# Attention scores and values side by side in 64x32 tiles of the matmul array

## The chip, the cores and the metric

The kernel runs on one core of a Trainium2 chip. The core has a matmul engine (TensorE, "PE" in the profile), three engines that read and write on-chip memory (VectorE "DVE", ScalarE "ACT", GpSimd "POOL") and a queue that issues DMA transfers (SyncE, "SP"). TensorE multiplies a stationary operand, loaded by an instruction of its own ("PEld", LDWEIGHTS), with a moving operand that streams through, and writes to PSUM, which has eight banks of 128 partitions x 512 float32. The metric is device time in microseconds (us), lower is better, as the median of several executions.

## The reference

The input x has 2048 rows of 640 features. Two attention blocks, A and B, with weights of their own, run on the same x; each has 32 heads of 20 features. A gate per row mixes the two results:

```
q, k, v = (x @ wqkv) split into 3 x 32 heads x 20
scores  = q @ k.T * 20 ** -0.5
p       = softmax(scores)
block   = (p @ v, heads side by side) @ wo
g       = sigmoid((x * gate_w).sum(-1))
out     = g * A + (1 - g) * B
```

## The kernel before

**Units of work.** The 64 heads of both blocks are taken in 16 groups of four (index g). A group has four blocks of 512 queries (qb), and each of these is worked off in eight steps of 256 keys. That makes `STEPS` = 16 x 4 x 8 = 512 steps, counted by G.

**Number formats.** Queries and keys stand as float16 in two parts (a high part and a remainder), so that a head takes 60 rows of 64: the rows of head pair members 0 and 1 lie in partitions 0 to 63 and 64 to 127 of the tiles `QT` and `KT`. Rows 60 to 63 carry the maximum of the scores of each query, subtracted inside the product. Values `V` and the weights of the softmax (`pt`) are float32.

**What a step does.** For step G the kernel issues

- scores (`scores`, "e" in the order below): 8 matmuls of 64 rows x 128 keys, with 512 queries moving (L696), each into a PSUM bank of its own; ScalarE takes the exponential of each bank into a `pt` tile (L699);
- maxima (`max_mm`, "m"): the same product the other way round for queries that come 15 steps later (`LEAD`): 8 matmuls of 60 rows x 128 queries with 512 keys moving (L638). VectorE reduces each bank to a maximum per query (L649). For one bank in eight, ScalarE first writes a part (L642), and VectorE combines it with another bank (L646);
- values (`values`, "V"), for the step before: two blocks, each of four float32 matmuls of 128 keys x 21 columns with 512 queries moving (L714). The four heads go to four column tiles of 32 columns and add up in one bank, `acc`;
- other products ("X", `slot`): the projections of the next groups (`project_a`, `project_r`: queries and keys; `project_v`: values) and the output projection (`out_tiles`), cut into blocks of 6 to 15 matmuls of the whole 128x128 array. All of them are issued by the helper `mms` at L426.

Two scores (or maxima) of the two halves of the rows run at the same time in two row tiles; the values use column tiles; the other products use the whole array.

**What sets the order.** Every engine works off its instructions in the order in which they were written. `STEP` (L54) spells that order out for a step: with no other block to place, with one, or with two when a deadline is near; `LATE` (L57) is for the last steps, in which no maxima are left. The functions `take`, `give`, `spend`, `tick_score` and `tick_block` keep a clock of estimated times, used only to choose which of the seven rotating banks (`NB`) a product gets. Generators in the list `side` are moved on by `advance`, once for each score; the DMAs that spread projected rows into `QT`, `KT` and `KD` are issued from such generators, paced by `PACE` (`spread`, `spread_differences`), all of them on the SP queue. `KD` holds differences of two halves of the keys, which the banks of L642/L646 use. After the last step of a query block `take_acc` takes `acc`, divides, and stores the result to a scratch in DRAM, from where `out_tiles` reads it.

**Values projected.** `project_v` computes the values of 128 keys for eight heads in one bank: 15 matmuls with 128 rows of x stationary and 160 columns of weights moving (161 for the first, with the gate), and ScalarE copies them into `V` (L592).

Of the kernel before, what the change touches and what calls it, by code (L numbers as in the profile page):

```python
# [11 lines left out]
F32 = mybir.dt.float32  # L12
I32 = mybir.dt.int32
AF = mybir.ActivationFunctionType
OP = mybir.AluOpType
# [19 lines left out]
VW = DH + 1  # L35
XE = 7
# [25 lines left out]
T_SCORE, T_MODE, T_VALUES, T_READY = 0.217, 0.1, 0.85, 0.39  # L62
# [9 lines left out]
def kernel(  # L72
# [36 lines left out]
    V = [consts.tile([P, NT, 2 * GH, VW], F32, name=f"v{i}") for i in range(2)]  # L109
# [43 lines left out]
    def tick_score(j, i):  # L153

        clock["pe"] = max(clock["pe"], rows_free[j], free_at[i])
        rows_free[j] = clock["pe"] + T_SCORE
        return clock["pe"] + T_READY
# [400 lines left out]

    def weights_v(gg):
# [15 lines left out]
        def split():  # L575
            hi, lo = v_tiles(gg)
            split_weights(st["t"], r_v[gg], hi[:, :, :160], lo[:, :, :160])
# [3 lines left out]
    def project_v(gg, j):  # L581

        wh, wl = blk["v", gg]
        w = 161 if gg == 0 else 160
        for u in range(2):
            if u and now[0] >= 0:
                yield
            n = slice((j + u) * P, (j + u + 1) * P)
            i, pt = take()
            yield from mms(i, pt[:, :w], [(a[:, c, n], b[:, c, :w]) for c in range(NC) for a, b in  # L590
                                          ((xh, wh), (xh, wl), (xl, wh))], 0.33)
            nc.scalar.activation(V[gg % 2][:, j + u, :, 0:DH], pt[:, :160].rearrange("p (h d) -> p h d", h=2 * GH),  # L592
                                 AF.Copy, scale=QKS)
            give(i, spend("act", 0.25, clock["done"]))
            v_done.add((gg, j + u))
            if gg == 0:
                nc.scalar.activation(gates[:, 0, j + u:j + u + 1], pt[:, 160:161], AF.Exp, scale=inv_g)
# [20 lines left out]
    def max_parts(g, qb):  # L618
        m = mparts[g, qb] = wts.tile([P, 2, 2, 4, 4], F32, name="mpart", tag="mpart", bufs=2)
        nc.gpsimd.memset(m[:, :, 0:1 if g else 2, :, 0] if g or qb >= AHEAD else m, LOW)  # L620

    def max_mm(u, ch, heads=(0, 1)):

# [7 lines left out]
        q0 = qb * QB + t * P  # L631
        for j in heads:
            two = u < AHEAD * NS or ch < 2 and (j == 0 or g == 0)
            i, pt = take()
            ready = tick_score(j, i)
            r = slice(64 * j, 64 * j + 60)
            k = KD[g % 2 if ch == 0 else 1][r, pair] if two and ch % 2 == 0 else KT[g % 2][r, pair, ch * QB:(ch + 1) * QB]
            nc.tensor.matmul(pt, QT[g % 2][r, pair, q0:q0 + P], k, start=True, stop=True)  # L638
            m = mparts[g, qb][:, pair, j, t, ch:ch + 1]
            if two and ch % 2 == 0:  # L640
                relus[u, j] = start.tile([P, QB], F32, name="rl0", bufs=4) if u < AHEAD * NS else work.tile([P, QB], F32, name="rl", bufs=2)
                nc.scalar.activation(relus[u, j], pt, AF.Relu)  # L642
                back = relu_at[u, j] = spend("act", T_EXP, ready)
            elif two:
                rl = relus.pop((u, j))
                nc.vector.tensor_tensor_reduce(rl, pt, rl, 1.0, LOW, OP.add, OP.max, m)  # L646
                back = spend("dve", T_MAX, max(ready, relu_at.pop((u, j))))
# [5 lines left out]
    def finish_max(g, qb):  # L653
# [18 lines left out]
        for h in range(GH):  # L672
            base, pair = 60 + 64 * (h % 2), h // 2
            nc.sync.dma_start(QT[g % 2][base:base + 4, pair, qb * QB:(qb + 1) * QB],
                              ms[:, 4 * h:4 * h + 4, :].rearrange("k t q -> k (t q)"))
# [12 lines left out]
    def scores(G, kk, pair, heads=(0, 1)):  # L688

        g, qb, i = unit_of(G)  # L690
        kt = 2 * i + kk
        for j in heads:
            i, et = take()
# [628 lines left out]
```

## Time and profile before

| | |
|---|---|
| median of 3 runs | 2743.61 us (2743.14 to 2743.99) |
| the profiled execution's own time (its span) | 2741.6 us |
| from the span's start to the first values | 103.6 us |
| TensorE busy, matmuls | 2725.5 us, 99%, 23333 instructions |
| TensorE busy, weight loads | 940.2 us, 34%, 23333 instructions |
| ScalarE busy | 2533.9 us, 92% |
| VectorE busy | 2426.1 us, 88% |
| GpSimd busy | 699.6 us, 26% |
| DMA | 125.59 MB, mean 46 GB/s |

How to read it: a row of a group names the line of the kernel, the engine, the operation, output and inputs, the shape, the count, busy time and the mean length of one instruction. A float32 matmul of the program stands in the trace as two, so the 4096 matmuls of L714 are 8192 records. Matmuls overlap: a record of 0.38 us can be followed by the next on the same tile after 0.22 us, so the pace is read from starts, not from lengths. The chain of waits names, for each moment, the work that the end of the kernel was waiting for.

### The profile page before, as it was taken

Reading aid. Unit: us, or ns where it says so; the run is one execution under the profiler, and the core shown is the slowest. Engines: PE = TensorE matmul, PEld = TensorE weight load, DVE = VectorE, ACT = ScalarE, POOL = GpSimd, SP = SyncE. Lnnn points to the kernel's source line nnn. Section 1 sums busy time; section 2 is a strip of 40 time slices with the busy share of each in tenths; the row PEclk is TensorE's granted clock in tenths of the full one; section 3 lists DMA queues with packets and bytes.
Section 4 is the critical chain, followed back from the end, with each engine's and each line's share of the span. In section 5 each row is a group of like instructions: output and inputs, shape, how many; then the busy total and the mean of one; then the engine's idle time right before and its main releaser. Section 6 shows DMA issues by size and latency. Waiting matters only on the chain.

```text
span 2741.6 us, 62441 instructions
## 1 busy us (share of the span) xinstructions
PE 2725.5 (99%) x23333; PEld 940.2 (34%) x23333; DVE 2426.1 (88%) x4712; ACT 2533.9 (92%) x5149; POOL 699.6 (26%) x1010
## 2 busy tenths in 40 slices
PE   9999999999999999999999999999999999999999
PEld 4433333333333332333333333333333333333222
DVE  8789999999999999888888998989988888999992
ACT  4999999999999999999999999999999999999997
POOL 6232222222223422312221121223342212211111
PEclk9999999999999999999999999999999999999999
DMA  4021102010120211102012230221201112122112
GB/s 144 17 59 24 31 15 44 7 33 14 25 55 20 61 45 51 39 9 61 20 49 53 67 85 25 60 57 47 67 17 42 29 51 64 32 77 62 49 49 77
DMA packets 175401, 125.59 MB, mean 46 GB/s; under 512 B 103672, under 2 KB 145456, under 8 KB 175096
## 3 DMA queue, kind: packets, MB, share of 16 engines
q1 hardware_dynamic: 172552, 120.31, 17.2%
q8 instruction: 182, 2.98, 0.4%
q0 software_dynamic: 1600, 0.96, 0.3%
q14 instruction: 123, 1.01, 0.1%
q10 hardware_dynamic: 944, 0.33, 0.0%
HBM read 55.53 MB, written 31.86 MB: 32 GB/s over the span
## 4 chain that ended last, share of the span: by engine, by line
PE 96%; ACT 1%; DVE 1%; issue 0%; DMA 0%; POOL 0%; POOLq 0%; SPq 0%; ACTq 0%; DVEq 0%
PE acc L714 36%; PE bank L426 21%; PE bank L638 20%; PE bank L696 18%; ACT pt L699 1%; DVE mpart L649 1%; PE bank L895 0%; PE bank L956 0%; PE acc L927 0%; DMA xs<-in_A_x_dram 0%; DVE rl L646 0%; ACT rl L642 0%; DVE ot L806 0%; POOL xx L899 0%; POOL on L875 0%
## 5 line engine op out<-in xcount | busy, mean ns | idle before, releaser
L699 ACT ACTIVATE pt<-bank 128x512 f32<-128x512 f32 x4096 | 2167.1, 613 | 125.8 <-PE bank L696 91.6
L649 DVE TENSOR_REDUCE mpart<-bank 128x1 f32<-128x512 f32 x2944 | 1842.2, 681 | 227.3 <-PE bank L638 122.7
L714 PE MATMUL acc<-pt,v 128*21 128x512 f32 x8192 | 1081.7, 600 | 0.1
L696 PE MATMUL bank<-qt,kt 64*128 64x512 f16 x4096 | 1035.2, 380 | 1.4 <-ACT pt L699 0.9
L638 PE MATMUL bank<-kt,qt 60*128 60x512 f16 x3520 | 1006.7, 380 | 1.4 <-ACT pt L699 0.2
L638 PEld LDWEIGHTS <-qt 60*128 60x128 f16 x4096 | 237.9, 94 | 896.7 <-issue 829.3
L646 DVE CUSTOM_DVE_ANT_0 rl<-bank,rl 128x512 f32<-128x512 f32 x576 | 386.5, 677 | 7.2 <-ACT rl L642 2.8
L642 ACT ACTIVATE rl<-bank 128x512 f32<-128x512 f32 x576 | 339.0, 598 | 7.3 <-PE bank L638 6.7
L714 PEld LDWEIGHTS acc<-pt,v 128*21 128x21 f32 x8192 | 143.0, 99 | 429.5 <-issue 426.5
L696 PEld LDWEIGHTS <-kt 64*128 64x128 f16 x4096 | 229.4, 94 | 174.1 <-issue 64.1
L426 PE MATMUL bank<-xx,wbh 128*128 128x168 f16 (+3 forms) x2480 | 286.4, 236 | 0.6 <-DVE xx L961 0.3
L426 PE MATMUL bank<-xx,wbl 128*128 128x168 f16 (+3 forms) x1240 | 257.5, 235 | 0.0
L426 PEld LDWEIGHTS <-wbh 128*128 128x128 f16 x2480 | 192.5, 98 | 110.2 <-issue 104.6
L814 POOL TENSOR_TENSOR ot<-ot,sq 128x512 f32<-128x512 f32 x63 | 66.1, 1049 | 574.7 <-DVE sq L811 539.4
L638 PE MATMUL bank<-kd,qt 60*128 60x512 f16 x576 | 203.4, 379 | 0.8
L426 PE MATMUL bank<-woh,o_in 128*128 128x320 f16 (+3 forms) x700 | 157.7, 290 | 0.0
L426 PE MATMUL bank<-wvh,xx 128*128 128x160 f16 (+1 forms) x1280 | 156.6, 234 | 0.0
L455 POOL CAST cq<-fs 128x512 f16<-128x512 f32 x60 | 36.7, 611 | 459.9 <-ACT fs L453 459.9
L426 PEld LDWEIGHTS <-xx 128*128 128x128 f16 x1920 | 131.1, 97 | 59.0 <-issue 56.2
L426 PE MATMUL bank<-wvl,xx 128*128 128x160 f16 (+1 forms) x640 | 137.7, 232 | 0.0
L426 PEld LDWEIGHTS <-wbl 128*128 128x128 f16 x1240 | 121.2, 98 | 4.7 <-issue 1.3
L426 PEld LDWEIGHTS <-o_in 128*128 128x128 f16 (+1 forms) x1050 | 87.3, 97 | 91.0 <-issue 68.5
(156 smaller groups left out, 1288.6 us busy)
## 6 DMA issues: line engine op xcount, KB each, us to landing
y_scr<-y_out SPq DMA_DIRECT2D x48, 320.0 KB
y_out<-y_scr SPq DMA_DIRECT2D x32, 320.0 KB
kt<-cq SPq DMA_DIRECT2D x120, 80.0 KB
o_scr<-on SPq DMA_DIRECT2D x240, 40.0 KB
o_in<-o_scr SPq DMA_DIRECT2D x64, 96.0 KB
kt<-cq SPq DMA_DIRECT2D x136, 40.0 KB
wstage<-in_B_wqkv_dram SPq DMA_DIRECT2D x13, 400.0 KB
xs<-in_A_x_dram SPq DMA_DIRECT2D x8, 640.0 KB
```

The source lines that it names most:

```text
L426: nc.tensor.matmul(out_ap, a, b, start=(k == 0), stop=(k == len(pairs) - 1))
L455: nc.gpsimd.tensor_copy(hi, f)
L638: nc.tensor.matmul(pt, QT[g % 2][r, pair, q0:q0 + P], k, start=True, stop=True)
L642: nc.scalar.activation(relus[u, j], pt, AF.Relu)
L646: nc.vector.tensor_tensor_reduce(rl, pt, rl, 1.0, LOW, OP.add, OP.max, m)
L649: nc.vector.tensor_reduce(m, pt, axis=AX.X, op=OP.max)
L696: nc.tensor.matmul(et, KT[g % 2][r, pair, kt * P:(kt + 1) * P], QT[g % 2][r, pair, qb * QB:(qb + 1) * QB], start=True, stop=True)
L699: nc.scalar.activation(pt, et, AF.Exp, scale=factor(g // 4))
L714: nc.tensor.matmul(acc[32 * h:32 * h + VW, :], V[(g // 2) % 2][:, kt, (g % 2) * GH + h, :], ptiles.pop((G, kk, h)), start=(kt == 0), stop= ...
L814: nc.gpsimd.tensor_tensor(t3, t3, sq.unsqueeze(2).to_broadcast([P, 16, 32]), op=OP.mult)
```

## The change

Every score, maximum and value matmul becomes a set of matmuls on tiles of 64 rows x 32 columns, of which the array has eight. A score bank no longer holds 128 keys of one head: it holds 64 keys of each of the two heads of a pair, the one head in partitions 0 to 63 and the other in 64 to 127. Each head needs two tiles (32 keys each), so a bank takes four matmuls on four of the eight tiles. The rows of member 1 (partitions 64 to 127) write to partitions 0 to 63 and those of member 0 to partitions 64 to 127, the two "crossed" quarters of the array. Maxima are built likewise, with 64 queries of two heads to a bank. In the first 16 units, which run before step 0, 64 columns at a time are used, and every other bank takes the uncrossed quarters.

The weights of the softmax for one head now lie in one half of the partitions, 64 keys at a time. The values of a head therefore use the rows of that half only, and write to the columns of the same half: the four tiles that the scores leave alone. A step has eight sets of four value matmuls over 256 queries each ("V" in the new order) in place of two sets over 512. The values of 64 keys must stand in the half of the partitions that belongs to the head: `project_v` computes each 64 keys for the two halves of the heads apart, in tiles of 128 rows x 64 columns: 60 matmuls of 80 columns in place of 15 of 160.

```diff
+HALF = QB // 2
+C = 64
+VB = 4 * DH
+CW = VB + 2
...
-STEP = ("e0 m0 m1 V m0 e1 e1 m0 m1 e1 e0 V e0 m1 m1 e0 e1 m0",
-        "X e0 m1 m0 e1 m0 m1 V m1 e0 e1 m0 e1 e0 V m0 e1 e0 m1",
-        "X m0 m1 e0 m1 e0 e1 V e1 e0 m1 m0 V e1 m0 m1 m0 e0 e1 X")
-LATE = "e0 e1 e0 e1 V X e0 e1 e0 e1 V"
+STEP = ("V m m V e e V m e V m e V m e V m e V e e V m m",
+        "V m m V e e V m e V m e V m e V m e V e e V m X m",
+        "V m X m V e e V m e V m e V m e V m e V e e V m X m")
+LATE = "V e V e V e V e V e V e V e V e"
...
+    def product_of_scores(pt, stationary, n, moving, swapped=False):
+
+        w = C if now[0] < 0 else 32
+        for j in (1, 0):
+            to = C * (j if swapped else 1 - j)
+            for c in range(0, C, w):
+                nc.tensor.matmul(pt[to + c:to + c + w], stationary(j)[:, n + c:n + c + w], moving(j), start=True, stop=True)
...
     def spread_differences(g, queues=repeat(nc.sync), to=None):
         dd = differences.pop(g)
-        for j in range(2 if g == 0 else 1):
+        for j in range(2):
...
     def project_v(gg, j):
...
+            for k in range(2):
+                n = slice((kc + k) * C, (kc + k) * C + C)
+                products = [(x, c, b) for c in range(NC) for x, b in ((xh, 0), (xh, 1), (xl, 0))]
+                for o, (x, c, b) in enumerate(products):
...
+                    for f in range(2):
+                        f0, f1 = (1 - (gg == 0), 1 + VB) if f else (1, 1 + VB + (gg == 0))
+                        to = C * (1 - f)
+                        nc.tensor.matmul(pt[to:to + C, CW * k + f0:CW * k + f1], x[:, c, n],
+                                         w[b][:, c, VB * f + f0 - 1 + f:VB * f + f1 - 1 + f], start=(k == o == 0),
+                                         stop=(k == 1 and o == len(products) - 1), skip_group_check=True)
...
-    def scores(G, kk, pair, heads=(0, 1)):
+    def scores(G, c, pair):
...
+        product_of_scores(et, lambda j: KT[g % 2][64 * j:64 * j + 64, pair], i0,
+                          lambda j: QT[g % 2][64 * j:64 * j + 64, pair, qb * QB:(qb + 1) * QB])
...
-    def values(G, kk):
+    def values(G, c, part):
         g, qb, i = unit_of(G)
-        tick_block(T_VALUES, weighed.pop((G, kk)))
-        kt = 2 * i + kk
+        tick_values(weighed[G, c])
+        kc = 4 * i + c
+        n = slice(part * HALF, part * HALF + HALF)
         for h in range(GH):
-            nc.tensor.matmul(acc[32 * h:32 * h + VW, :], V[(g // 2) % 2][:, kt, (g % 2) * GH + h, :],
-                             ptiles.pop((G, kk, h)), start=(kt == 0), stop=(kt == NT - 1))
+            r = slice(C * (h // 2), C * (h // 2) + C)
+            nc.tensor.matmul(acc[32 * h:32 * h + VW, n], V[(g // 2) % 2][r, kc, (g % 2) * 2 + h % 2, :],
+                             ptiles[G, c, h % 2][r, n], start=(kc == 0 and part == 0),
+                             stop=(kc == S // C - 1 and part == 1), skip_group_check=True)
```

The rest follows from the new layout: `V` has 32 pieces of 64 keys and four heads to a half of the partitions; the split of the value weights into high and low parts on GpSimd is done in two halves (one more CAST and one more subtraction for each group of values); the maxima of a query block are laid out by halves of 64 queries, and the DMAs that bring them back into rows 60 to 63 of `QT` move pieces of 64 queries (two DMAs for each head in place of one for the first two blocks); `head_at` gives the order of the four heads in `acc`; `KD` is filled for both members of a pair in every group; the clock of estimates gets `tick_values`.

More of the change, by code (lines that the diff above doesn't have):

```diff
@@ L108 @@
     KD = [consts.tile([P, 2, QB], F16, name=f"kd{i}") for i in range(2)]
-    V = [consts.tile([P, NT, 2 * GH, VW], F32, name=f"v{i}") for i in range(2)]
+    V = [consts.tile([P, S // C, GH, VW], F32, name=f"v{i}") for i in range(2)]
     acc = psum.tile([P, QB], F32, name="acc")
@@ L1230, with one_max @@
     half_done = set()
-    def one_max(u, ch, j):
-        max_mm(u, ch, (j,))
+    def one_max(u, ch, s):
+        max_mm(u, ch, (s,))
         if u % NS == NS - 1 and ch == ORDER[3]:
@@ L1252 @@
             for u, ch in next_maxima(G, 1):
-                for j in (1, 0):
-                    one_max(u, ch, j)
+                for s in range(2):
+                    one_max(u, ch, s)
             finish_step()
@@ L1274 @@
                     out_tasks(G)
-            elif what[0] == "m":
-                for u, ch in some[(k - 1) * len(some) // 4:k * len(some) // 4]:
-                    one_max(u, ch, int(what[1]))
+            elif what == "m":
+                for one in some[(k - 1) * len(some) // 8:k * len(some) // 8]:
+                    one_max(*one)
             elif what == "V":
-                product()
+                if k % 4 == 0:
+                    product()
                 if G:
-                    values(G - 1, k - 1)
-                    if G % NS == 0 and k == 2 and G < STEPS:
+                    values(G - 1, (k - 1) // 2, (k - 1) % 2)
+                    if G % NS == 0 and k == 8 and G < STEPS:
                         side.append(take_acc(*unit_of(G - 1)[:2]))
```

138 lines of the change are left out of this document (85 added, 53 removed).

## The prediction

> **What bounds the kernel now.** I read the page's busy times first, then the chain of waits, then one step of the chain, then the timeline inside it.
>
> ```profile
> span 2741.6 us, 62441 instructions
> PE 2725.5 (99%) x23333; PEld 940.2 (34%) x23333; DVE 2426.1 (88%) x4712; ACT 2533.9 (92%) x5149; POOL 699.6 (26%) x1010
> PE 96%; ACT 1%; DVE 1%; issue 0%; DMA 0%; POOL 0%; POOLq 0%; SPq 0%; ACTq 0%; DVEq 0%
> ```
>
> The end waits for TensorE 96% of the time. ScalarE and VectorE are not far behind, which matters below. One step of the chain (start, length, work):
>
> ```profile
> 1301.34 0.99 PE acc L714 x8
> 1302.32 0.32 PE bank L638
> 1302.86 1.19 PE bank L426 x15
> 1304.06 0.32 PE bank L696
> 1304.82 0.98 PE acc L714 x8
> 1305.80 0.32 PE bank L638
> 1306.56 0.99 PE acc L714 x8
> ```
>
> From 1301.34 to 1306.56 the step takes 5.22 us: values 0.99, scores 0.54 (to 1302.86), a block of other products 1.19, scores 0.76, values 0.98, scores 0.76. Now what the six stretches are made of:
>
> ```profile
> 1300.51 0.39 PE L638 MATMUL bank<-kt,qt 60*128 60x512 f16 x1
> ...
> 1300.74 0.38 PE L638 MATMUL bank<-kt,qt 60*128 60x512 f16 x1
> 1300.96 0.38 PE L696 MATMUL bank<-qt,kt 64*128 64x512 f16 x2
> ...
> 1301.27 0.14 PEld L714 LDWEIGHTS acc<-pt,v 128*21 128x21 f32 x8 [0.43 <-issue]
> 1301.27 1.06 PE L714 MATMUL acc<-pt,v 128*21 128x512 f32 x8
> ```
> ```profile
> 1301.27 0.63 PE L714 MATMUL acc<-pt,v 128*21 128x512 f32 x4
> ```
> ```profile
> L714 PE MATMUL acc<-pt,v x8192: 592/593/609, 103.6 to 2727.5; 128*21 128x512 f32 x200
> ```
>
> Scores follow each other on a tile every 0.22 us (1300.51, .74, .96), two banks at a time. The values' eight records last 1.06, the first four of them 0.63; with lengths of 0.609 and 0.593 the second four begin 0.445 later. So a V block streams for 2 x 0.44 = 0.88 and ends in about 0.10 before the next kind can start; from the last score to the first value there are 1301.27 - 1300.96 - 0.22 = 0.09. Each of the six changes of kind in a step costs about 0.10: 16 scores 8 x 0.22 = 1.76, values 1.77, block 1.09, changes 0.60, together 5.22.
>
> **What the change removes.** Scores and values now have the same tile form and separate quarters of the array, so four of the six changes go. Only the two around the block stay. What it costs: a score bank (four matmuls on half the array) takes the place of half a pair, so the 16 banks need 16 x 0.22 in a lane of their own; the values, with 64 keys and half the queries to a matmul, need 16 float32 passes in the other lane. The lanes run abreast, in 16 slots. A slot is as long as a score (0.22) or as half of today's pass: 0.445/2 = 0.222 if all of it scales, or 0.231 if the 0.018 that a pass takes beyond two scores' streams of 0.2135 (0.445 - 0.427) stays per record. I take 0.225, near the row of the scores: 3.60 (3.52 to 3.70). With two changes 3.80 (3.72 to 3.90), against 1.76 + 1.77 + 0.60 = 4.13. **Gain 0.33 us a step with a block (0.23 to 0.41).** The new order writes one set of values, then two scores, and a score has to be written behind the values' second pass; this shifts the score lane by one slot and costs nothing as long as the order keeps two scores to a V, as it does through the whole of a full step.
>
> ```profile
> L426 PE MATMUL bank<-wvh,xx 128*128 128x160 f16 x1120 | 136.6, 234 | 0.0
> L426 PE MATMUL bank<-wvl,xx 128*128 128x160 f16 x560 | 120.1, 231 | 0.0
> ...
> L426 PE MATMUL bank<-xx,wbh 128*128 128x128 f16 x960 | 91.7, 220 | 0.1
> L426 PE MATMUL bank<-xx,wbl 128*128 128x128 f16 x480 | 85.3, 219 | 0.0
> ```
> ```profile
> 267.40 1.15 PE bank L426 x15
> ```
> ```profile
> 241.62 0.94 PE bank L426 x15
> ```
>
> These groups are those of the main part (from 105 us on), and the two pieces of the chain a block of 160 and one of 128 columns. There are 1680 / 15 = 112 blocks of projected values, and, counted step by step in the timeline, about 480 of the 512 steps hold some block. So 368 steps without projected values gain 368 x 0.33 = **121 us** (85 to 151).
>
> **Projected values.** A block of 160 columns took 1.15, less 0.10: 0.070 a matmul. It becomes 30 pairs of 80 columns, each pair on two column tiles at once, with a load of 64 columns before each matmul. No row shows this. Below, a pair is half of today's 0.070: 0.035. Above: in a 128-column block matmuls follow every (0.94 - 0.10)/15 = 0.056, and a load of 128 columns keeps up with that, so two loads of 64, even one behind the other, should need no more than 0.056. I take 0.046, between the two: 1.38 us a block (1.05 to 1.68), 0.33 more than now. In these 112 steps gain and cost cancel: **0 us** (46 gained to 45 lost). The 16 blocks before the first step add 5 (0 to 10).
>
> On the Trainium skill, "TensorEngine Tiling (Array Packing)", Restrictions and Gotchas, and "TensorE: Matmul & The Clock Gate", LDWEIGHTS: column tiling turns the fast weight load off, and a load takes its columns divided by 1.2 ns. By that, 64 columns take 53 ns, a pair 53 ns with loads abreast and 107 ns one behind the other; the sum would be 24 us above mine, or 205. The rows' 128 columns inside 56 ns are loads with the fast path on, so they don't contradict it.
>
> **What takes over.** TensorE gets faster, ScalarE and VectorE do the same work.
>
> ```profile
> 105.00:2666.00 2561.00, 2558.06 (x22140) 866.22 (x22138) 2318.80 (x4460) 2410.08 (x4893) 637.10 (x902) 1.00 0.17 43
> ```
> ```profile
> L699 ACT ACTIVATE pt<-bank 128x512 f32<-128x512 f32 x4096 | 2167.1, 613 | 125.8 <-PE bank L696 91.6
> L649 DVE TENSOR_REDUCE mpart<-bank 128x1 f32<-128x512 f32 x2944 | 1842.2, 681 | 227.3 <-PE bank L638 122.7
> ```
> ```profile
> 1300.97 3.04 ACT L699 ACTIVATE pt<-bank 128x512 f32<-128x512 f32 x6 [0.20 <-PE bank L696]
> ...
> 1304.45 2.48 DVE L649 TENSOR_REDUCE mpart<-bank 128x1 f32<-128x512 f32 x4 [0.33 <-PE bank L638]
> ```
>
> Of 2561 us VectorE is busy 2319 and ScalarE 2410 (columns: PE, PEld, DVE, ACT, POOL; clock 1.00). In a row ScalarE takes (3.04 - 0.61)/5 = 0.49 a bank, VectorE (2.48 - 0.68)/3 = 0.60. A step of nine ScalarE banks is then 4.4 us and with its copies 4.6; VectorE's seven or so 0.60 and the rest come to about the same. The step that TensorE would need, 3.80 + 1.09 = 4.89, is only 6% longer. TensorE works in order: one bank not yet freed stops both lanes. I charge **35 us** (0 to 70) for steps in which one of the two is late.
>
> **Small parts.** The 15 later groups send four more DMAs each into `KD` (now `kd<-dd SPq`):
>
> ```profile
> kd<-dd SPq DMA_DIRECT2D x38, 40.0 KB
> kd<-dd SPq DMA_DIRECT2D x30, 20.0 KB
> ```
>
> They stand on the SP queue ahead of the next group's keys and delay those by a step or so, paced as they are; the 15 steps by which maxima run ahead cover it. Without that cover maxima bunch up, and VectorE is late next: some 3 us a group, 45 in all, the upper part of the 35 (0 to 70). The halved pieces of the maxima's DMAs have the same cover. GpSimd, 26% busy, hides the added splits. The last steps, without maxima, stay with ScalarE (55.77 busy of the last 60 us):
>
> ```profile
> 2666.00:2726.00 60.00, 59.88 (x451) 16.24 (x450) 16.90 (x34) 55.77 (x112) 5.93 (x9) 1.00 0.23 73
> q8 instruction: 182, 2.98, 0.4%
> ```
>
> The matmul records rise from 23333 to about 78,000 (values 32,768, scores and maxima 32,500, projected values 7,680, the rest 5,030), with as many loads. Their code comes over the queue q8 in pieces of 16 KB, 256 instructions, 0.004 x 16 x 2741.6 / 182 = 0.96 us each: one every 15 us now, one every 4.5 us then, still hidden by the instructions in hand; if not, 610 x 0.96 = 590 us.
>
> **Sum.** 2741.6 - 121 + 0 + 5 + 35 = 2660.6 of a span; the median of the runs lies 2.0 above the profiled span, so **2663 us**. With the ends: 2741.6 - 197 = 2545, which ScalarE's 2410 busy of 2561 makes unlikely below 2590; and 2741.6 + 40 = 2782.
>
> **Rivals.** (1) ScalarE and VectorE give nothing back: they are 94% and 91% busy, and seven banks may be too few to keep both fed. For it:
>
> ```profile
> ACT pt L699 <- PE bank L696: 91.6, 385, 0.8
> DVE mpart L649 <- PE bank L638: 122.7, 271, 8.6
> ```
>
> only 91.6 of ScalarE's and 122.7 of VectorE's idle us were waits of this kind, about 0.2 and 0.5 us each. Against it: these waits are what the change shortens, since banks arrive evenly and no longer in bursts between blocks of values. Then the saved changes become waits for banks: 2740 us (2725 to 2760). (2) Slower, from the loads of `project_v`: if a pair can't start before its 64-column load is done, the recorded length of a load is the nearest price:
>
> ```profile
> L426 PEld LDWEIGHTS <-wbh 128*128 128x128 f16 x2480 | 192.5, 98 | 110.2 <-issue 104.6
> ```
>
> 30 x 0.098 = 2.94 us a block, 1.56 above mine, x 128 blocks = 200: 2863 us. It decides from the block at which 128 x (block - 1.38) eats the gain of 81: 2.01 us, a pair of 67 ns. Against it: in full-size blocks loads of 98 ns hide behind matmuls 56 ns apart. (3) TensorE can't be fed: a step has 94 loads and matmuls now (32 + 32 + 30) and 286 then (128 + 128 + 30), 376 with projected values. From 5.2/286 = 18 ns an instruction this decides. The trace shows eight loads started within 0.14 - 0.10 = 0.04 us out of a full queue, so about 3 ns with the matmuls between, and 28 ns in the long run of the 128-column blocks, where streaming is the limit. At 28 ns: 8.0 us a step, 105 + 512 x 8.0 = 4200 us. On the Trainium skill, "Runtime: NRT & Kernel Launch", Instruction fetch mechanics: the sequencer issues an instruction in about 20 cycles, which at the 1.2 GHz that the page on TensorE gives for it is 16.7 ns (an estimate). That gives 4.8 us for 286, no loss, and 6.3 for 376: 112 x 1.1 more, 2786 us. No run here shows it. (4) The change doesn't do what it says: two halves of the rows may not stream into one bank at once. In the trace two row tiles always write to different banks (the two L696 at 1300.96 have one each by the program). Then every slot counts double: 7.2 + 1.3 = 8.5 us, 4450 us.
>
> **How the numbers follow.** Forecast 0.60 (own range 2600 to 2725); rival 1 0.13, about half of it within 0.2% of before, which is what a measurement here can tell from no change; rival 2 0.14; rival 3 0.08; rival 4 0.05. Faster: 0.60 + 0.06 = 0.66; same 0.06; slower 0.28. The range of 2590 to 2790 takes in the upper end of the sum and rival 1, and below stops where ScalarE does.
>
> **What would show it.** Right: the step's chain has no 0.99 pieces of values any more, records of scores and values start abreast, each every 0.22 to 0.23 us; a step with a 128-column block falls from 4.13 + 0.84 = 4.97 to about 4.7; idle time before L699 and the reductions shrinks. A block of projected values much over 1.7 us shows rival 2; ScalarE or VectorE with 20% or more of the chain, rival 1; spacing of matmuls without any wait inside a slot, rivals 3 or 4. It would be wrong if values and scores start one after another.

## The result and the profile after

The changed kernel takes **2718.31 us** (median of 4 runs, 2715.22 to 2726.63) against 2743.68 us before it in the same comparison (2743.14 to 2743.99): a ratio of 0.9912, 95% interval 0.9896 to 0.9928. It is faster by 25 us. The forecast was 2663 us, 81 less than before: the sign was right, and so was what the change does to TensorE's order of work, but two thirds of the forecast gain are missing.

The profiled execution is the slowest of the four (2726.63 us, span 2724.8). First its page: busy times, the chain by engine, the two engines that read the banks, and the queue that brings the code.

```profile
span 2724.8 us, 176719 instructions
PE 2667.3 (98%) x77989; PEld 1624.3 (60%) x77989; DVE 2400.0 (88%) x4713; ACT 2493.5 (92%) x5165; POOL 700.5 (26%) x1025
q8 instruction: 609, 9.98, 1.6%
PE 85%; ACT 7%; DVE 3%; issue 3%; DMA 1%; POOL 1%; ACTq 0%; SPq 0%; POOLq 0%; DVEq 0%
L758 ACT ACTIVATE pt<-bank 128x512 f32<-128x512 f32 x4096 | 2068.0, 634 | 29.7 <-PE bank L170 26.9
L704 DVE TENSOR_REDUCE mpart<-bank 128x1 f32<-128x512 f32 x2944 | 1864.7, 681 | 224.4 <-PE bank L170 184.8
L697 ACT ACTIVATE rl<-bank 128x512 f32<-128x512 f32 x576 | 342.9, 605 | 120.0 <-PE bank L170 107.0
```

Of the chain, which was TensorE for 96%, ScalarE now holds 7%, VectorE 3% and "issue", time in which TensorE waits for nothing that the profile shows, 3%. The idle time ahead of the exponentials fell from 125.8 to 29.7 us, but ahead of VectorE's reductions it stayed (227.3 before, 224.4 now), and ahead of the ReLU of L697 120.0 are idle, where the kernel before had 7.3:

```profile
L642 ACT ACTIVATE rl<-bank 128x512 f32<-128x512 f32 x576 | 339.0, 598 | 7.3 <-PE bank L638 6.7
```

The array does what the change says. In the timeline of TensorE (start, length) scores or maxima (L170) and values (L779) start abreast, every 0.22 us:

```profile
1301.68 0.39 PE L170 MATMUL bank<-kd,qt 60*32 60x512 f16 x4
1301.70 0.40 PE L779 MATMUL acc<-pt,v 64*21 64x256 f32 x4
1301.90 0.39 PE L170 MATMUL bank<-kt,qt 60*32 60x512 f16 x4
1301.91 0.40 PE L779 MATMUL acc<-pt,v 64*21 64x256 f32 x4
...
1302.77 0.39 PE L170 MATMUL bank<-qt,kt 64*32 64x512 f16 x4
1302.78 0.40 PE L779 MATMUL acc<-pt,v 64*21 64x256 f32 x4
```

From 1301.68 to 1302.77 lie five slots: 0.218 us each, so 16 take 3.49. Where a score bank comes free in time nothing else is left in a step: 16 slots, a block, two changes.

Two views show what eats the gain. The chain of waits at an early block of projected values (L637):

```profile
766.45 1.01 PE bank L637 x46
767.45 0.92 issue
768.37 0.41 PE bank L637 x12
...
772.74 1.23 PE bank L637 x56
```

The block at 772.74 runs through in 1.23 us; the one at 766.45 stops in its middle for 0.92, with all its operands there and no semaphore to wait for. And ScalarE and VectorE in one step without projected values (timeline; in brackets the idle time before):

```profile
1301.65 0.39 ACT L472 ACTIVATE fs<-bank 128x168 f32<-128x168 f32 x1
1302.19 0.60 ACT L697 ACTIVATE rl<-bank 128x512 f32<-128x512 f32 x1
1302.70 4.03 ACT L758 ACTIVATE pt<-bank 128x512 f32<-128x512 f32 x8
1306.58 0.56 ACT L849 ACTIVATE y_out<-bank,f_o 128x320 f32<-128x320 f32 x1
```
```profile
1306.99 2.48 DVE L704 TENSOR_REDUCE mpart<-bank 128x1 f32<-128x512 f32 x4 [0.72 <-PE bank L170]
```

From its copy at 1301.65 to the next at 1306.58 ScalarE needs 4.93 us and stands idle only between the copy and the ReLU (1302.19 - 1301.65 - 0.39 = 0.15): here the step is as long as ScalarE's work. VectorE gets a pause of 0.72 once a step, behind the block.

Step times, from the first value record of a step to that of the next, taken from the timeline (medians in us by what block the step holds; "halves" are the experiments below, with half of the exponentials and maxima left out):

| step with | before | before, halves | after | after, wide products | after, wide products and halves |
|---|---|---|---|---|---|
| 128 columns projected (96 steps) | 4.97 | 4.97 | 4.87 | 4.87 | 4.54 |
| 168 columns projected (93) | 5.22 | 5.22 | 5.02 | 5.03 | 4.79 |
| projected values (110, after 108) | 5.18 | 5.18 | 5.27 (mean 5.40) | 4.85 (mean 4.97) | 4.75 |
| output projection (130, after 127) | 5.17 | 4.97 | 5.01 | 5.02 | 4.70 |

### The profile page after: what moved, and what is told of

Its sections match the earlier page's. It is cut to its first block, busy times and chain, and to the rows that moved or that the text cites. A ratio compares the mean times of both kernels' runs of the same rounds, so it can differ in the third digit from the quotient of the medians.

```text
span 2724.8 us, 176719 instructions
## 1 busy us (share of the span) xinstructions
PE 2667.3 (98%) x77989; PEld 1624.3 (60%) x77989; DVE 2400.0 (88%) x4713; ACT 2493.5 (92%) x5165; POOL 700.5 (26%) x1025
## 4 chain that ended last, share of the span: by engine, by line
PE 85%; ACT 7%; DVE 3%; issue 3%; DMA 1%; POOL 1%; ACTq 0%; SPq 0%; POOLq 0%; DVEq 0%
PE bank L170 46%; PE acc L779 17%; PE bank L445 15%; ACT pt L758 6%; PE bank L637 6%; DVE mpart L704 2%; DMA ws<-in_A_wqkv_dram 0%; PE bank L963 0%; DMA xs<-in_A_x_dram 0%; ACT rl L697 0%; DMA kt<-mrow 0%; DVE rl L701 0%; DVE ot L874 0%; DVE mneg L711 0%; ACTq L758 0%
## 5 line engine op out<-in xcount | busy, mean ns | idle before, releaser
L758 ACT ACTIVATE pt<-bank 128x512 f32<-128x512 f32 x4096 | 2068.0, 634 | 29.7 <-PE bank L170 26.9
L704 DVE TENSOR_REDUCE mpart<-bank 128x1 f32<-128x512 f32 x2944 | 1864.7, 681 | 224.4 <-PE bank L170 184.8
L779 PE MATMUL acc<-pt,v 64*21 64x256 f32 x32768 | 1974.3, 378 | 9.2 <-issue 5.7
L170 PE MATMUL bank<-qt,kt 64*32 64x512 f16 x16384 | 1389.2, 378 | 17.4 <-issue 3.6
L170 PE MATMUL bank<-kt,qt 60*32 60x512 f16 (+1 forms) x13952 | 1377.5, 379 | 6.2 <-issue 3.3
L779 PEld LDWEIGHTS acc<-pt,v 64*21 64x21 f32 x32768 | 831.3, 97 | 85.3 <-issue 27.4
L170 PEld LDWEIGHTS <-kt 64*32 64x32 f16 x16384 | 504.0, 92 | 383.1 <-issue 164.2
L170 PEld LDWEIGHTS <-qt 60*32 60x32 f16 (+1 forms) x16128 | 495.2, 91 | 384.0 <-issue 133.4
L697 ACT ACTIVATE rl<-bank 128x512 f32<-128x512 f32 x576 | 342.9, 605 | 120.0 <-PE bank L170 107.0
L170 PE MATMUL bank<-kd,qt 60*32 60x512 f16 (+1 forms) x2176 | 209.5, 378 | 1.0 <-issue 0.6
L637 PEld LDWEIGHTS <-xx 128*64 128x64 f16 x7680 | 153.9, 110 | 55.3 <-issue 52.8
L637 PE MATMUL bank<-wvh,xx 128*64 128x80 f16 (+1 forms) x5120 | 171.9, 202 | 5.4 <-issue 4.7
L637 PE MATMUL bank<-wvl,xx 128*64 128x80 f16 (+1 forms) x2560 | 159.4, 201 | 2.1 <-issue 2.0
```

Source lines behind the costliest of these rows:

```text
L170: nc.tensor.matmul(pt[to + c:to + c + w], stationary(j)[:, n + c:n + c + w], moving(j), start=True, stop=True)
L637: nc.tensor.matmul(pt[to:to + C, CW * k + f0:CW * k + f1], x[:, c, n], w[b][:, c, VB * f + f0 - 1 + f:VB * f + f1 - 1 + f], start=(k == o ...
L697: nc.scalar.activation(relus[u, s], pt, AF.Relu)
L704: nc.vector.tensor_reduce(m, pt, axis=AX.X, op=OP.max)
L758: nc.scalar.activation(pt, et, AF.Exp, scale=factor(g // 4))
L779: nc.tensor.matmul(acc[32 * h:32 * h + VW, n], V[(g // 2) % 2][r, kc, (g % 2) * 2 + h % 2, :], ptiles[G, c, h % 2][r, n], start=(kc == 0 a ...
```

## The experiments

Two theories stood against each other for the missing gain. **Supply:** TensorE runs out of instructions. If the records of TensorE (loads and matmuls) of the changed kernel are numbered in their order, the stops without a releaser stand at one count in every 256, a count that drifts slowly, from 169 at the first stops to 131 at the last; 256 records are one piece of code on the queue q8 (155,978 records, 609 pieces). There are some 85 such stops over 0.3 us in the main part, about 50 us together, some 45 us of it where the last 256 records contain projected values. **Banks:** ScalarE and VectorE give banks back late, and TensorE, which works in order, stops both lanes.

**1. Projected values in wide products.** In the main part:

```diff
-            for k in range(2):
-                n = slice((kc + k) * C, (kc + k) * C + C)
...
+                n = slice((j + u) * P, (j + u + 1) * P)
...
+                    nc.tensor.matmul(pt[:, :2 * VB], x[:, c, n], w[b][:, c, :].rearrange("p (f w) -> p f w", w=VB + 1)[:, :, :VB], start=(o == 0), stop=(o == len(products) - 1))
+                nc.scalar.activation(V[gg % 2][:, kc:kc + 2, :, 0:DH], pt[:, :2 * VB].rearrange("p (k n d) -> p k n d", k=2, d=DH),
+                                     AF.Copy, scale=QKS)
...
```

> Everything of the changed kernel, but in the main part the projected values are formed as before, by 15 full-array products of 160 columns into 128 keys of one bank and one copy, instead of by 60 products of 128x64 and 80 columns. The values then stand in the wrong half of the partitions for half of the heads, so the result is another one; every instruction that reads them is unchanged. Supply theory (TensorE runs dry at fixed counts of its instructions when 256 of them are used up in under about 3.6 us, 52 us in all, 48 of them with projected values among the last 256): falls by 40 to 50 us, to about 2672, the steps with projected values from 5.40 to about 4.95 us, and the stops without a releaser from 52 to under 10 us. ScalarE theory (every step is held at about 4.9 us by ScalarE's queue anyway): falls by 10 us at most.

Measured: 2666.84 us (2665.85 to 2667.46), ratio to before 0.9719 (0.9703 to 0.9735). That is 51.5 us less, all that the supply theory asked for. Waits of TensorE by what ended them (us in total, times, longest), first the changed kernel's, then this one's:

```profile
PE bank L170 <- issue: 7.6, 16, 1.7
PE bank L637 <- issue: 6.8, 16, 1.1
PE acc L779 <- issue: 5.7, 14, 1.1
```
```profile
PE acc L789 <- issue: 0.7, 1, 0.7
...
PE bank L170 <- issue: 0.3, 1, 0.3
```

This view counts only what the modelled ends of the matmuls before a stop leave visible, 20.1 us in 46 stops; now 1.0 in two. In the table only the steps with projected values change; the other kinds stay where they were. A block in the chain of this kernel:

```profile
764.10 1.16 PE bank L631 x15
```

It takes 1.16 us against the 1.23 of 60 products: 0.07 x 112 = 8 us of the 51.5 are the block itself, the other 44 the stops.

The transfer times of the pieces on q8 in the changed kernel's trace say what a stop waits for. In all of 64 such stops with projected values TensorE goes on 1.2 to 1.6 us after a piece has landed, which is 2.2 to 3.2 us after its transfer began, and the transfer of the next piece begins 1.0 us after that or later. So in the main part two transfers never begin closer together than 3.34 us, although one takes only about 1.06 us. That spacing is the limit, not the length of a transfer.

**2. to 4. Less work for ScalarE, for VectorE, for both.**

```diff
-        nc.scalar.activation(pt, et, AF.Exp, scale=factor(g // 4))
+        nc.scalar.activation(pt[:, :HALF], et[:, :HALF], AF.Exp, scale=factor(g // 4))
...
-                nc.vector.tensor_reduce(m, pt, axis=AX.X, op=OP.max)
+                nc.vector.tensor_reduce(m, pt[:, :HALF], axis=AX.X, op=OP.max)
...
```

> The changed kernel with the exponential taken over 256 of a bank's 512 columns; the values read the first 256 columns twice. Half of the exponentials are left out, TensorE's and VectorE's instructions are as many and as long as they were. ScalarE theory (the scores wait for ScalarE to give banks back, about 130 us of the 172 us of such waits): falls by 90 to 130 us, to about 2610. Rival (VectorE's maxima or TensorE's instruction supply hold the steps): falls by less than 30 us.

> The changed kernel with VectorE's maxima taken over 256 of a bank's 512 columns, so the maxima leave half of the scores out; ScalarE as it was. VectorE theory (its reductions give the banks back late): falls by 90 us or more. ScalarE theory: falls by 15 to 45 us, what the traces show of waits that VectorE ends or shares (15 and 33 us).

> The changed kernel with both left out, half of the exponentials and half of the maxima: TensorE with banks always free. If waits for banks are what is missing: falls by about 170 us to 2550, with the stops of the instruction supply (52 us or more, since TensorE then runs faster) left over. If the array's halves themselves take longer than the slots of 0.22 us say (a lower clock, a conflict): stays above 2650.

Measured: half the exponentials 2666.86 us (51 less than the changed kernel), half the maxima 2712.19 (6 less, hardly to be told from none), both 2605.39 (113 less, where 170 were expected). For the first neither branch of the expectation held, and the second gave less than either of its branches: ScalarE is the larger part, but with ScalarE relieved VectorE takes over after 51 us, and only both together give the 113. So it is not one engine. The chain with half the exponentials, and with both halves:

```profile
PE 94%; DVE 2%; issue 1%; DMA 1%; POOL 1%; ACT 0%; SPq 0%; POOLq 0%; DVEq 0%; ACTq 0%
```
```profile
PE 95%; issue 1%; DMA 1%; POOL 1%; DVE 1%; ACT 0%; SPq 0%; POOLq 0%; DVEq 0%; ACTq 0%
```

**5. The same halves in the kernel before the change.** The edit is that of experiment 4.

> The kernel before the change with half of the exponentials and half of the maxima left out (the values read the first 256 columns of each exponentiated tile twice), the counterpart of the same edit on the changed kernel, which took 113 us from it. If ScalarE and VectorE became the limit only through the change: the kernel before falls by less than 20 us, since TensorE was busy 97 percent of its span. If they held the kernel before as well: it falls by 50 us or more.

Measured: 2719.66 us (2719.4 to 2720.93), 24 us less: somewhat over the 20 of the first theory. The medians of the steps with projections stay as they were; what gets shorter is outliers, the steps with a block of the output projection (5.17 to 4.97) and the few steps without a block. The page has TensorE as busy as ever, with the other two at 58% and 64%:

```profile
PE 2703.7 (99%) x23333; PEld 917.5 (34%) x23333; DVE 1585.9 (58%) x4712; ACT 1731.4 (64%) x5149; POOL 699.3 (26%) x1010
```

So of the 113 us that banks cost the changed kernel, 113 - 24 = 89 came with the change.

**6. The 60 products alone, in the kernel before.**

```diff
-            yield from mms(i, pt[:, :w], [(a[:, c, n], b[:, c, :w]) for c in range(NC) for a, b in
-                                          ((xh, wh), (xh, wl), (xl, wh))], 0.33)
...
+                for f in range(2):
+                    for o, (a, c, b) in enumerate(products):
+                        for k in (1, 0):
+                            to = 64 * k
+                            nc.tensor.matmul(pt[to:to + 64, 80 * f:80 * f + 80], a[:, c, (j + u) * P + to:(j + u) * P + to + 64],
+                                             b[:, c, 80 * f:80 * f + 80], start=(f == o == 0),
...
```

> The kernel before the change with one part of it alone: in the main part the projected values of 128 keys are formed by 60 products of 128x64 and 80 columns instead of 15 of 128x128 and 160 columns; scores, values and every copy as before, the result the same. Supply theory (a limit on the pace of instructions, of 256 in about 3.6 us): a step with projected values has 184 instructions of TensorE in 5.2 us, far from the limit, so the time stays within 10 us of before. Rival (60 short products are slow in themselves, by loading 60 stationaries): each of the 112 blocks takes over 0.4 us more, 45 us or more in all.

Measured: 2749.75 us, 6 us more than before (ratio 1.0021, 1.0012 to 1.0031). A step with projected values goes from a median of 5.18 to 5.24 us. The same 60 products that cost 51.5 us beside the new scores and values cost 6 beside the old ones, with 184 instead of 376 of TensorE's instructions in the step. It is the pace that costs, not the products.

**7. Both causes taken away.** Wide products (experiment 1) and both halves (experiment 4).

> The changed kernel with projected values by 15 wide products (wrong half of the partitions for half of the heads) and with half of the exponentials and of the maxima left out: neither instruction supply nor banks should be late. If the two causes are separate, their gains add up: 2718 less 113 less 51 is 2554 us. If they hide each other, it stays well above, toward 2590; if there is a third limit, the steps without a block of X stay above 3.9 us.

Measured: 2533.91 us (2530.72 to 2535.78), 20 below the 2554 of the two gains added up, which neither branch had: there are two causes, each of which hides some 20 us of the other. With banks free the supply costs more (2605.39 - 2533.91 = 71.5) than with banks late. This is TensorE's own floor: 0.43 us a step below the kernel before with its halves in the first three rows of the table, 0.27 in the fourth. Another queue enters the chain here, SP's, which issues the DMAs of the projected rows:

```profile
PE 95%; SPq 2%; DMA 1%; POOL 1%; issue 0%; DVE 0%; ACT 0%; POOLq 0%; DVEq 0%; ACTq 0%
```

**8. A version for use.** The wide products put the values of half of the heads into the wrong partitions; GpSimd moves them.

```diff
-                nc.scalar.activation(V[gg % 2][:, kc:kc + 2, :, 0:DH], pt[:, :2 * VB].rearrange("p (k n d) -> p k n d", k=2, d=DH),
-                                     AF.Copy, scale=QKS)
+                vs = work.tile([P, QB], F32, name="fs")[:, :2 * VB]
+                nc.scalar.activation(vs, pt[:, :2 * VB], AF.Copy, scale=QKS)
+                for k in range(2):
+                    for f in range(2):
+                        to = slice(C * (1 - f), C * (1 - f) + C)
+                        nc.gpsimd.tensor_copy(V[gg % 2][to, kc + k, :, 0:DH],
+                                              vs[C * k:C * k + C, VB * f:VB * f + VB].rearrange("p (n d) -> p n d", d=DH))
```

> The changed kernel with the projected values in 15 wide products and one ScalarE copy into a staging tile, from which GpSimd moves four pieces of 64 partitions and 80 columns to the half of the partitions where the values read them. The result is the kernel's own. If GpSimd's 448 moves of some 0.25 us stay hidden (it is busy 26 percent): as fast as the kernel with wide products alone, about 2667 us, faster than both kernels. If the values wait for the moves: above 2680, with waits for GpSimd ahead of the value products.

Measured: **2667.02 us** (2666.53 to 2669.7), ratio to before 0.9722 (0.9706 to 0.9738): the gain of experiment 1 with the whole computation in place, faster than both kernels. Its group of moves and its idle ScalarE:

```profile
L638 POOL COPY v<-fs 64x80 f32<-64x80 f32 x448 | 112.4, 251 | 257.3 <-ACT fs L633 237.3 <-DMA o_in<-o_scr 2.7
```
```profile
L773 ACT ACTIVATE pt<-bank 128x512 f32<-128x512 f32 x4096 | 2065.8, 635 | 22.1 <-PE bank L170 19.8 <-ACT rl L712 1.9
L712 ACT ACTIVATE rl<-bank 128x512 f32<-128x512 f32 x576 | 343.0, 605 | 98.9 <-PE bank L170 78.3
L472 ACT ACTIVATE fs<-bank 128x168 f32<-128x168 f32 (+2 forms) x240 | 86.2, 359 | 4.3 <-PE bank L445 2.5 <-issue 0.3
L633 ACT ACTIVATE fs<-bank 128x160 f32<-128x160 f32 x112 | 39.9, 356 | 2.7 <-issue 1.2 <-PE bank L631 1.0 <-POOL on L904 0.6
```

448 moves at 0.251 us keep GpSimd busy for 112 us that no other engine waits for.

**9. to 11. Can ScalarE's share be had back?** An order with a score bank behind the block, copies shared with VectorE, and both, on top of version 8:

```diff
-        "V m m V e e V m e V m e V m e V m e V e e V m X m",
-        "V m X m V e e V m e V m e V m e V m e V e e V m X m")
+        "V m m V e e V m e V m e V m e V m e V e m V m X e",
+        "V m X m V e e V m e V m e V m e V m e V e m V m X e")
```
```diff
+        by[0] = ("act", "dve")[next(copies) % 2]
+        if by[0] == "dve":
+            nc.vector.tensor_scalar(to, at, QKS, None, op0=OP.mult)
+        else:
+            nc.scalar.activation(to, at, AF.Copy, scale=QKS)
...
+        return spend(by[0], 0.35, clock["done"])
...
-                nc.scalar.activation(f[:, m], pt[:, m], AF.Copy, scale=QKS)
-                give(i, spend("act", 0.25, clock["done"]))
+                copy_by(f[:, m], pt[:, m])
+                give(i, copy_done())
...
```

The second edit also raises the clock's estimate of a copy from 0.25 to 0.35 us, and with it changes which bank a product gets.

> The kernel with wide products moved by GpSimd (2667 us), and in the steps with a block of X the last score bank placed behind the block instead of ahead of it, a maximum in its old place: ScalarE then finds an exponential's bank 0.22 us earlier after the block's copy, where it stood idle for about 0.12 us a step. If ScalarE's queue sets the step: 370 steps by 0.1 us, 25 to 40 us less. If the gap is only slack that comes back elsewhere (VectorE, whose bank is then later): within 8 us.

> The kernel with wide products moved by GpSimd (2667 us), with every second copy of projected queries, keys and values out of its bank on VectorE instead of ScalarE. If ScalarE's queue is the limit (0.39 us of copy, 0.50 of the ReLU and 8 exponentials at 0.48 in steps of 4.85 us) and VectorE has room: ScalarE's work per step falls by 0.2 us on the mean, 40 to 70 us less. If VectorE, 88 percent busy, then holds the banks instead: within 10 us of 2667 or above it.

> Both of these edits together. If both relieve the same queue of ScalarE: at least the better of the two, and the sum of both gains where TensorE's own floor (about 4.54 to 4.80 us a step, 2534 us without waits) isn't reached: 2590 to 2620. If VectorE takes over: no better than the better one alone.

Measured: 2723.47, 2693.74 and 2732.11 us: 56, 27 and 65 **more** than version 8. The first lies outside both branches of its expectation; for the other two the branch in which VectorE takes over had the direction, but not, as shown below, the cause. ScalarE's groups with the score behind the block:

```profile
L773 ACT ACTIVATE pt<-bank 128x512 f32<-128x512 f32 x4096 | 2119.6, 644 | 75.4 <-PE bank L170 48.3 <-ACT pt L773 1.6 <-ACT rl L712 1.4
L712 ACT ACTIVATE rl<-bank 128x512 f32<-128x512 f32 x576 | 342.2, 604 | 9.1 <-PE bank L170 7.2
L472 ACT ACTIVATE fs<-bank 128x168 f32<-128x168 f32 (+2 forms) x240 | 72.0, 300 | 38.6 <-PE bank L445 29.8 <-issue 4.9 <-POOL on L903 0.4
L633 ACT ACTIVATE fs<-bank 128x160 f32<-128x160 f32 x112 | 34.1, 304 | 27.2 <-PE bank L631 18.7 <-issue 6.5 <-POOL ot L897 0.7
```

The wait ahead of the ReLU went (98.9 to 9.1), as meant, but ScalarE now runs dry before the block's copy (4.3 + 2.7 to 38.6 + 27.2) and ahead of the exponentials (22.1 to 75.4). The bank that was moved behind the block was one of those that fed ScalarE through it. With shared copies the wait ahead of the ReLU grows instead:

```profile
L726 ACT ACTIVATE rl<-bank 128x512 f32<-128x512 f32 x576 | 342.4, 604 | 152.9 <-PE bank L170 143.5
```

ScalarE has less to do and waits longer for the ReLU's bank (98.9 to 152.9).

Which engine keeps TensorE waiting can be read bank by bank, since `take` fixes the bank of each product when the program is built. In version 8 the score and maximum banks that directly follow another begin 130 us late in all (those over 0.04 us late, against slots of 0.22), and 126 us of it end 0.05 us after the instruction that read the same bank: 111 us ScalarE's, 15 VectorE's. With the score behind the block it is 191 us, 70 ScalarE's and 106 VectorE's. With shared copies it is 149 us, 139 ScalarE's and 6 VectorE's: VectorE does not give banks back late there. What grew are the waits during which another bank stood free, from 57 to 90 us, so the changed choice of banks is a rival to the sharing itself; no run separates the two. Neither edit relieved TensorE, and a third theory took the place of "ScalarE is the wall": what is short is the **stock of full banks**.

**12. One bank fewer.** Version 8 with six of the seven rotating banks from the first step on.

```diff
-        i = min((k for k in range(NB) if k not in held), key=lambda k: free_at[k])
+        i = min((k for k in range(NB if now[0] < 0 else NB - 1) if k not in held), key=lambda k: free_at[k])
```

> The kernel with wide products moved by GpSimd (2667 us), with six of the seven rotating banks used from the first step on; every instruction is the same. If ScalarE's work alone sets the step (it is always fed, 4.85 us a step): within 15 us of 2667. If the steps depend on a stock of full banks, with which ScalarE and VectorE get through the 1.2 us of a block in which TensorE fills none: one bank fewer is 0.5 us of work for one of them in each of some 480 steps, 60 to 240 us more.

Measured: 2778.81 us (2778.42 to 2780.27), 112 more, with the same instructions. ScalarE waits more in its midst:

```profile
L712 ACT ACTIVATE rl<-bank 128x512 f32<-128x512 f32 x576 | 341.2, 601 | 151.4 <-PE bank L170 143.7 <-DVE mpart L719 2.4
L472 ACT ACTIVATE fs<-bank 128x168 f32<-128x168 f32 (+2 forms) x240 | 76.9, 321 | 20.8 <-PE bank L445 12.1 <-issue 2.2 <-POOL on L903 0.9
```

A bank is worth 112 us, in the range that the stock theory gave. Read bank by bank, the banks begin 247 us late in place of 130, 118 more. During a block and its changes, some 1.2 us, TensorE fills no score bank, while ScalarE takes one in 0.49 us and VectorE one in 0.60, together 1 / 0.49 + 1 / 0.60 = 3.7 in a microsecond, or 4.4 in a block (an estimate from these rows). The traces show the stock at both ends of a block: in version 8, 5.5 of the seven banks hold scores or maxima on the mean when a block begins, which takes one itself, and when the first bank behind it is begun, at 410 of 476 blocks no full one is left that isn't being read. With six banks it is 4.9 at the start, and none is left at 431 of 453. So the stock fills up nearly to the limit between blocks, and a block uses it up: TensorE waits for free banks ahead of it, and the readers for full ones behind it. The seven banks can't be made more: the eighth holds `acc`.

## Why the prediction was right and where it was wrong

What happened between 2743.6 and 2718.3 us, by these runs:

| | us | from |
|---|---|---|
| TensorE's own work, with wide products and banks free | -185.8 | 2719.7 to 2533.9, both with halves |
| projected values in 60 products, stops among them | +71.5 | 2533.9 to 2605.4, both with halves |
| late banks that the change brought | +89.0 | 2605.4 to 2718.3 is 112.9, less 23.9 that they cost before |
| together | -25.3 | 2743.6 to 2718.3 |

The last two sizes depend on the order: taken with banks late, the 60 products cost 51.5 (experiment 1), and the late banks are then 109.

The missing 55 us are, by size, the term for late banks: 35 forecast, 89 measured. TensorE's terms add up to 116 us gained in the forecast (121 less 5) and to 114 in the runs (2719.7 to 2605.4, both with halves), but that is luck: the slots and changes gained some 70 us more than forecast, and the 60 products, put at about nothing, took 71.5 back.

**Slots and changes: right, a little too careful.** Slots came out at 0.218 instead of 0.225, and with the changes still at 0.10 each that is 16 x 0.218 + 0.20 = 3.69 instead of 3.80, just under the lower end of 3.72; with the 0.84 of a block of 128 columns it makes 4.53, and the step measures 4.54 with banks free. So the step is 4.97 - 4.54 = 0.43 shorter, not 0.33; the range of 0.23 to 0.41 ended just below. Rivals 4 (halves of the rows one after another) and 2 (loads exposed) are false: slots start abreast, and a block of projected values takes 1.23 us, not 2.94.

**Projected values: the term was wrong in both directions.** The block costs 1.23 in place of 1.15, 0.08 more and not 0.33: less 0.10 for its change of kind that is 0.038 for a pair, where I took 0.046 between 0.035 and 0.056. By this alone these 112 steps would have gained some 0.35 us each. They lost instead (5.21 to 5.40 on the mean; 4.97 with the stops gone), by the stops, for which the prediction had no term.

**The step "still hidden by the instructions in hand" failed: nothing charged, 44 to 64 us measured** (the 51.5 to 71.5 of the 60 products less 8 for the longer block). I worked out a piece of 256 instructions every 4.5 us on the average of the kernel and compared it with the 0.96 us that a piece takes on its queue. What decides is the stretch with the most instructions, and the spacing at which pieces can follow one another, which was never under 3.34 us. A step with projected values has 376 of them, so at the 4.85 us of experiment 1 it would use up 256 in 3.3 us. In the changed kernel's trace, groups of 256 records used up in under 3.3 us are followed by a stop in about two thirds of the cases, those of 3.6 to 4.0 us in 15%, those over 4.0 in about 1%. The limit is so about 256 in 3.6 us, or 14 ns an instruction, and 376 x 14 ns = 5.3 us is the length of such a step after the change. Rival 3 came near it, with a chance of 0.08: it had TensorE short of instructions, but as a pace of each single one, with the point at 18 ns, not as the spacing of pieces of code; in its milder form it belonged into the sum, at about 50 us. The Trainium skill, "Runtime: NRT & Kernel Launch", Instruction fetch mechanics, says that fetching is hidden since the sequencer issues no faster than about every 20 cycles; the stops at every 256th record and their end in experiment 1 say otherwise for this kernel.

**"What takes over" failed on size: 35 us charged, 89 measured.** I compared work with work, 4.6 us of ScalarE's in a step of 4.89, and let 6% of room stand as nearly enough. Both engines have that little room, are fed through seven banks in order and lose their supply for a block each step; the stock of banks bridges the block only in part (experiment 12). Relieving either alone gives less than both: half the exponentials 51, half the maxima 6, both 113. The upper bound of 70 was too low as well. What the prediction held against rival 1, that banks arriving evenly would shorten the waits, came true ahead of the exponentials (125.8 to 29.7) but not ahead of the reductions (227.3 to 224.4), and ahead of the ReLU it went the other way (7.3 to 120.0). Rival 1 has this mechanism; it let the waits eat all of TensorE's gain, and they ate about half of it (89 of 186).

**Small parts.** The last steps do not "stay with ScalarE". ScalarE in the last steps before and after:

```profile
2702.32 6.04 ACT L699 ACTIVATE pt<-bank 128x512 f32<-128x512 f32 x12 [0.38 <-PE bank L696]
2708.73 2.07 ACT L699 ACTIVATE pt<-bank 128x512 f32<-128x512 f32 x4 [0.38 <-PE bank L696]
```
```profile
2678.38 4.03 ACT L758 ACTIVATE pt<-bank 128x512 f32<-128x512 f32 x8 [1.60 <-PE bank L170]
2682.98 4.03 ACT L758 ACTIVATE pt<-bank 128x512 f32<-128x512 f32 x8 [0.58 <-PE bank L170]
```

Without maxima the lane of the scores is half empty, but the values still take their 16 slots, 3.5 us, where two sets of 0.88 us stood before; a block comes on top, and ScalarE waits 0.6 to 1.6 us a step. The last 32 steps went from 148 to 160 us. The start cost 4 us (first values at 107.7 instead of 103.6), near the 5 forecast. That the added `KD` transfers, the extra splits and the halved pieces of the maxima's DMAs cost nothing was not tried by itself; no wait for them of over 1 us in total stands in the waits of TensorE.

## What to carry to other kernels

When a change cuts work into more and smaller instructions, take the instruction count of the densest stretch, not of the kernel, and compare its pace with the spacing at which pieces of code follow one another at their fastest (3.34 us here), not with the length of one transfer (1.06 us); blocks of 60 small products undid 51 us here, and four copies on an engine that was 26% busy gave them back. When the bound engine gets faster and the next two stand at 90%, busy shares don't tell what is left: cut the work of each and of both in an experiment, since they share the banks and their losses don't add. A gap in the order of an engine that feeds others through a few buffers is paid for by the buffers that are full when it begins; before moving work across the gap, count them.

## What the runs showed that was not expected

- TensorE stops for want of instructions without any sign among the waits but "issue": some 85 stops over 0.3 us, about 50 us in all, at one slowly drifting place in every 256 records, from a pace of about 14 ns an instruction. Pieces of 256 follow one another at 3.34 us or more, though one transfer takes about 1.06. 60 products of 80 columns in 1.23 us are 120 instructions at 10 ns, so short stretches may be faster; only the sum over 256 counts.
- Four matmuls of two halves of the rows write to two halves of the partitions of one bank at once, in a slot of 0.218 us, no longer than one matmul over 128 columns took before (0.22). The Trainium skill, "TensorEngine Tiling (Array Packing)", Restrictions and Gotchas, states that different row tiles can't access one bank at the same time; with separate partitions of the bank these rows show them abreast.
- Pairs of 128x64 tiles of 80 columns follow one another every (1.23 - 0.10) / 30 = 0.038 us, although the load ahead of each product is recorded with 0.110 us:

```profile
L637 PEld LDWEIGHTS <-xx 128*64 128x64 f16 x7680 | 153.9, 110 | 55.3 <-issue 52.8
```

- One of seven PSUM banks is worth 112 us of 2667 in a kernel in which three engines are busy 90 to 99%.
